# A fused RWKV5 and feed-forward kernel: packing the first chunks' k, staging w2 apart, and a new order

## The chip, the cores and the metric

The kernel runs on one core of one Trainium2 chip. A core has five engines with queues of their own: TensorE (matmul and transposes), VectorE, ScalarE, GpSimd, and SyncE, which mostly issues transfers; ScalarE issues transfers too. Each engine takes its instructions in the order of the program and waits on semaphores where another engine or a transfer has to come first. The metric is the time of the whole kernel on the device in microseconds, as the median of several runs; a profiled execution stands beside it.

## The reference

A linear attention with a decaying state (4 batches, 8 heads, 768 tokens, head size 48), then a layer norm and a feed-forward block with a residual over the 8 x 48 = 384 channels:

```python
for t in range(S):
    cur = einsum('bhd,bhe->bhde', u * k_t, v_t)
    y[:, :, t] = einsum('bhd,bhde->bhe', r_t, state + cur)
    state = w * state + einsum('bhd,bhe->bhde', k_t, v_t)
x = y as (B, S, 384)
xn = (x - mean(x)) / sqrt(var(x) + 1e-6) * g_ln
out = x + relu(xn @ w_ch1) @ w_ch2        # 384 -> 1536 -> 384
```

All inputs and the output are float32.

## The kernel before

The 768 tokens of each batch are cut into 6 chunks of 128, so there are 24 chunks. Inside a chunk the recurrence is done as attention: r is scaled by powers of w that grow with the token's place and k by powers that shrink, a matrix of products of r and k is masked to the lower triangle, and the state is carried from chunk to chunk. Each step of a chunk is a short function. For chunk i:

- LK, LV load k and v with a token to a partition (pieces of 192 bytes, one for each head and token); RA and RB load the two halves of r "packed", four tokens to a partition (pieces of 768 bytes), for chunks 0 to 17; LR loads r like k after that.
- SK and SR scale k and r into the bf16 tile `sc`, with the factors Fk and Fr (Fn for the later r). CV makes v bf16 (`vv`).
- TR transposes both on TensorE (four transposes for r, four for k), TCr and TCk copy the results from PSUM to `trs`; the copy of the packed r puts the tokens back in order. From chunk 14 on transfers transpose k (TKD), from 18 on both (TKR).
- Q multiplies the two turned tiles; AT makes the products of r and k for the eight heads, AM (or AMa and AMb, its halves) masks them on VectorE into `A`.
- S makes, on TensorE, the part with u and the state's new terms from `sc` and `vv`; CC copies the former, ZU and ZD form the decayed state Z. VB multiplies v by CC's result (`Vb`).
- Y puts together the output from Z and A; X adds Vb and sums over the channels; SQ and RS make the norm's factor; XN makes the normalised bf16 row.
- LT and XT turn it on TensorE for chunks 0 to 5; LT2 and LTD turn it by transfer later.

The feed-forward part works on groups of one or two chunks: UP is one PSUM bank's share of the first product (12 matmuls of 128 columns or 6 of 256), RL its ReLU into `hT` (on ScalarE or VectorE), DN a third of the second product (4 matmuls), OT the residual, STO the store. The last chunk's second product goes in two halves (DA, DB, OA, OB, SA, SB).

The weights arrive as float32. LW1 loads a third of w_ch1 into `w1_f`, SW scales it by the norm's g to bf16. LW2 loads a third of w_ch2 into the same memory, through w2_f, so it waits until SW has read it; CW makes it bf16. DU is a dummy matmul of 512 columns on TensorE, which keeps it busy while it has nothing else to do.

In the setup LC loads w, u and g_ln as rows, LN takes the logarithm, CT and CP turn the rows into columns, WBR and WBK spread the logarithms over the partitions by matmul, PW makes the exponents, and FK, FN and FR make the factors by exponentials on ScalarE, FR in four instructions.

The order is written out by hand as a long string, PLAN: each word names a step, its chunk (or part), and its engine (v VectorE, s ScalarE, g GpSimd, - the step's own; for transfers s is ScalarE's queue and - SyncE's). The steps are issued in that order, so every engine's queue has the order of its own words in the string. A tile with several buffers is a ring: chunk i takes buffer i modulo the number in SLOTS.

```python
for step in PLAN.split():
    name, i, e = step.split(",")
    steps[name](int(i), e)
```

Transfers signal their landing on eight semaphores in turn, so an issuing engine, before it issues, waits until the transfer that had the same semaphore before has landed.

Of the kernel before, what the change touches and what calls it, by code (L numbers as in the profile page):

```python
# [18 lines left out]
PLAN = """
MW,0,v LC,0,s TL,0,s MM,0,g DU,4,- LK,1,- LK,0,- MI,0,g DU,4,- DU,4,- RA,1,s DU,4,- LC,1,- LK,2,- RB,1,- LV,0,- LN,0,s  # L20
RB,0,s WBR,0,- DU,4,- BD,0,g LV,3,- DU,4,- PW,0,v MP,0,v FR,3,s FR,1,s WBK,0,- RA,0,s DU,4,- FR,2,s FR,0,s RA,2,s LV,1,-
LK,3,- DU,4,- DU,4,- LC,2,s DU,4,- SR,1,g DU,4,- DU,4,- FK,0,s SK,0,v FN,0,s SR,0,v RB,2,s LV,2,- SK,1,v LW1,1,s CT,0,-
TR,0,- LW1,0,- RA,3,s SK,2,v DU,4,- DU,4,- TCr,0,s LW1,2,- DU,4,- CP,0,v DU,4,- TCk,0,v UW,0,g CV,0,g TR,1,- Q,0,v SR,2,g
TCk,1,s DU,4,- S,0,- DU,4,- CC,0,s WL,0,s UGC,0,s RA,4,- DU,4,- SK,3,g CV,3,g TCr,1,s DU,4,- DU,4,- VB,0,g AT,0,- DU,4,-
SW,5,s TR,2,- CV,1,s Q,1,g ZU,0,v AMb,0,v AMa,0,v LK,4,- RB,5,- Y,0,- TCr,2,s RB,3,s X,0,v SW,4,s XN,0,s SW,3,v TCk,2,v
DU,4,- AT,1,- S,1,- DU,4,- CC,1,v DU,4,- VB,1,g AMa,1,v DU,4,- ZU,1,v RB,4,- DU,4,- LW2,1,- DU,4,- DU,4,- SW,2,s CV,2,s
SQ,0,s DU,4,- AMb,1,v LT,0,- SW,1,v Q,2,v DU,4,- AT,2,- Y,1,- SW,0,s SR,3,v XT,0,v DU,4,- LW2,0,s S,2,- TR,3,- UP,0,-
AMb,2,v DU,4,- SW,7,g SW,6,g CC,2,v TCr,3,s SW,8,s TCk,3,s DU,4,- AMa,2,v ZU,2,v RA,5,- DU,4,- DU,4,- RL,0,v X,1,v XN,1,s
UP,2,- LW2,2,- VB,2,g LK,5,- UP,1,- Q,3,g RL,2,v LV,4,- RB,6,- RA,6,- LT,1,- Y,2,- CW,1,s RL,1,s XT,1,v AT,3,- X,2,v
UP,17,- UP,16,- S,3,- AM,3,v XN,2,g CW,0,g RS,0,g RL,17,s LT,2,- Y,3,- RL,16,v CC,3,v XT,2,s UP,18,- SQ,1,s VB,3,v UP,32,-  # L30
RL,18,s X,3,v DN,0,- RL,32,s XN,3,v ZU,3,v SR,4,v UP,33,- CW,2,s CW,3,v LT,3,- UP,34,- RL,33,s XT,3,s SR,5,v DN,1,- SK,4,v
CW,5,s RL,34,s TR,4,- LK,6,- CW,4,v UP,48,- TCk,4,v SQ,2,s RB,8,s DN,2,- SK,5,g RS,1,g TCr,4,v UP,49,- OT,0,v RB,7,- Q,4,v
RA,7,s TR,5,- AT,4,- CV,4,v LV,5,- LK,7,- RA,8,- LV,6,- AM,4,v DN,4,- TCk,5,s S,4,- TCr,5,s RL,48,s SR,6,g DN,5,- RA,10,s
SQ,3,s Q,5,v Y,4,- CC,4,v SK,6,v DN,6,- ZU,4,v VB,4,g TR,6,- OT,1,v LK,8,- LV,7,- AT,5,- UP,50,- RS,3,g RL,49,s TCk,6,s
TCr,6,s X,4,v DN,8,- XN,4,g AM,5,v SR,7,g S,5,- LT,4,- DN,9,- XT,4,s RB,9,s CV,6,s RS,2,g LK,9,- RA,9,- AT,6,- SK,7,v
SQ,4,s UP,65,- DN,10,- RL,50,s Q,6,v CC,5,v CV,5,g SR,8,g RB,10,- LK,10,- S,6,- TR,7,- Y,5,- AM,6,v OT,2,v RL,65,s CC,6,v
VB,5,v UP,64,- RA,11,s TCr,7,s VB,6,g X,5,v DN,12,- STO,0,s CV,7,s TCk,7,v Y,6,- XN,5,g SQ,5,s ZU,6,v DN,13,- Q,7,v RL,64,s
LT,5,- RA,12,- SK,8,v RS,5,g AT,7,- S,7,- XT,5,v DN,14,- UP,66,- ZU,7,v SR,9,g X,6,v UP,81,- TR,8,- RL,66,s ZD,7,g AM,7,v
# [121 lines left out]

# [558 lines left out]
```

## Time and profile before

| | us |
|---|---|
| median of 3 runs | 155.74 |
| lowest, highest | 155.28, 156.29 |
| the profiled execution | 156.69 |
| its span, from first to last instruction | 154.9 |

The profile's times count from the start of the span, in us unless marked ns; the names of engines in it are PE for TensorE (PEld its weight loads), DVE for VectorE, ACT for ScalarE, POOL for GpSimd and SP for SyncE; SPq and ACTq are transfers issued by these. A row of the timeline has start, length, engine, line, operation, tiles with shapes and the number of instructions merged; square brackets say how long the engine had been idle before and what ended that. Rows can overlap by some tens of nanoseconds, because an instruction begins before the last has quite ended. A row of the groups has the busy time, the mean in ns, and after the second bar the idle time before these instructions with what ended it.

The whole span by engine: TensorE is busy 94% of it, VectorE 74%, GpSimd 58%, ScalarE 52%; transfers move 27.74 MB at 179 GB/s on average.

### The profile page before, as it was taken

The numbers are of one execution on the slowest core, as the hardware profiler recorded it, in microseconds if no ns is written. First come the engines' busy times: TensorE is split into PE (matmuls) and PEld (weight loads), VectorE is DVE, ScalarE is ACT, GpSimd is POOL, SyncE is SP. The second block draws the span as 40 slices with busy tenths as digits, with TensorE's granted clock in tenths as the row PEclk, the third lists the DMA queues.
The fourth block names the chain that finished last, engine by engine and source line by source line (L and its number), as shares of the span: only waits on it lengthen the run. The fifth ranks groups of instructions, "written<-read, shape, count | busy, mean of one in ns | idle before, by whom it ended". The sixth has DMA issues, their size and how long they took to land.

```text
span 154.9 us, 4408 instructions
## 1 busy us (share of the span) xinstructions
PE 145.7 (94%) x1744; PEld 110.4 (71%) x1744; DVE 115.4 (74%) x235; ACT 81.0 (52%) x183; POOL 89.3 (58%) x131
## 2 busy tenths in 40 slices
PE   4969899999999999999999999999999999799992
PEld 1326457897778877878887778688777878578881
DVE  0252499799899998997778989995984788496411
ACT  4321794686668387564996047862516631036130
POOL 5314763665288998796299596599634269403100
PEclk9999999999999999999999999999999999999999
DMA  4999989969989317969999969899998876521122
GB/s 92 231 242 305 368 223 295 276 147 223 189 199 254 78 30 174 230 190 207 225 142 208 138 153 223 204 222 112 253 213 179 161 165 106 146 78 30 51 102 102
DMA packets 82401, 27.74 MB, mean 179 GB/s; under 512 B 73035, under 2 KB 80846, under 8 KB 82382
## 3 DMA queue, kind: packets, MB, share of 16 engines
q1 hardware_dynamic: 77788, 21.96, 68.1%
q10 hardware_dynamic: 4594, 5.51, 11.8%
q8 instruction: 13, 0.21, 0.5%
q14 instruction: 6, 0.05, 0.1%
HBM read 18.88 MB, written 4.72 MB: 152 GB/s over the span
## 4 chain that ended last, share of the span: by engine, by line
PE 54%; DMA 13%; issue 10%; DVE 8%; POOL 7%; SPq 2%; ACT 2%; ACTq 1%; POOLq 0%; DVEq 0%
PE o L615 19%; PE hp L587 16%; PE o L304 4%; DMA rf<-in_r_dram 4%; DMA out_dram<-ot 4%; DMA trs<-sc 3%; PE at L435 3%; POOL sc L211 3%; DMA xT<-xn 3%; PE tr L415 2%; PE tr L419 2%; DVE sc L211 2%; PE y L516 2%; POOL rs L547 1%; PE s L479 1%
## 5 line engine op out<-in xcount | busy, mean ns | idle before, releaser
L587 PE MATMUL hp<-xT,w_sb 128*128 128x128 bf16 (+1 forms) x612 | 57.3, 242 | 1.0 <-DMA xT<-xn 0.8
L615 PE MATMUL o<-w_sb,hT 128*128 128x384 bf16 x276 | 55.6, 326 | 0.6 <-DVE ot L671 0.3
L587 PEld LDWEIGHTS <-w_sb 128*128 128x128 bf16 x612 | 48.6, 114 | 6.2 <-DMA xT<-xn 1.5
L603 ACT ACTIVATE hT<-hp 128x512 bf16<-128x512 f32 x55 | 32.4, 596 | 39.4 <-PE hp L587 36.9
L615 PEld LDWEIGHTS <-hT 128*128 128x128 bf16 x276 | 23.9, 97 | 11.1 <-issue 0.9
L445 DVE TENSOR_TENSOR A<-at,mask 128x1024 bf16<-128x1024 f32 (+1 forms) x27 | 29.5, 1097 | 1.6 <-PE at L435 1.3
L671 DVE SCALAR_TENSOR_TENSOR ot<-o,rs,x 128x384 f32<-128x384 f32 x23 | 14.1, 614 | 10.4 <-PE o L615 8.2
L498 POOL TENSOR_TENSOR Vb<-vf,cc 128x384 f32<-128x384 f32 x15 | 13.4, 891 | 13.4 <-DVE cc L208 10.3
L206 ACT COPY trs<-tr 128x512 bf16<-128x512 bf16 x22 | 12.4, 586 | 13.1 <-PE tr L419 13.1
L211 POOL TENSOR_TENSOR sc<-kf,Fk 128x384 bf16<-128x384 f32 x12 | 12.8, 1073 | 6.4 <-issue 2.9
L530 ACT ACTIVATE sqj<-x,sm 128x384 bf16<-128x384 f32 x24 | 14.8, 617 | 2.0 <-DVE x L523 1.6
L523 DVE SCALAR_TENSOR_TENSOR x<-y,Vb 128x384 f32<-128x384 f32 x24 | 13.2, 550 | 2.8 <-PE y L516 1.4
L211 POOL TENSOR_TENSOR sc<-rf,Fr 128x384 bf16<-128x384 f32 x13 | 13.7, 1057 | 2.3 <-DMA rf<-in_r_dram 2.3
L304 PE MATMUL o<-warm 128*128 128x512 bf16 x36 | 13.8, 508 | 1.1 <-DVE warm L259 1.1
L605 DVE TENSOR_SCALAR hT<-hp 128x512 bf16<-128x512 f32 x17 | 11.5, 686 | 2.4 <-PE hp L587 2.2
L547 POOL TENSOR_TENSOR rs<-rs,expo 128x1 f32<-128x1 f32 (+1 forms) x17 | 11.2, 662 | 1.4
L211 DVE TENSOR_TENSOR sc<-kf,Fk 128x384 bf16<-128x384 f32 x12 | 8.3, 701 | 3.1 <-ACT Fk L319 3.1
L211 POOL TENSOR_TENSOR Z<-ZS,WLZ 128x384 bf16<-128x384 f32 x8 | 8.3, 1043 | 3.6 <-DVE ZS L492 3.6
L211 POOL TENSOR_TENSOR q<-trs 128x512 bf16<-128x512 bf16 x7 | 8.4, 1200 | 3.3 <-DMA trs<-sc 2.4
L435 PE MATMUL at<-trs 48*128 48x128 bf16 x192 | 9.5, 219 | 0.3 <-DVE A L445 0.2
L435 PEld LDWEIGHTS <-trs 48*128 48x128 bf16 x192 | 5.4, 94 | 5.7 <-issue 3.8
L516 PE MATMUL y<-vv,A 128*128 128x48 bf16 x192 | 8.7, 183 | 0.5 <-DVE A L445 0.5
(90 smaller groups left out, 190.3 us busy)
## 6 DMA issues: line engine op xcount, KB each, us to landing
kf<-in_k_dram SPq DMA_DIRECT2D x24, 192.0 KB, 3.9
vf<-in_v_dram SPq DMA_DIRECT2D x24, 192.0 KB, 4.2
w_f<-in_moe_w_ch_dram SPq DMA_DIRECT2D x4, 768.0 KB, 6.3
out_dram<-ot ACTq DMA_DIRECT2D x12, 192.0 KB, 3.2
out_dram<-ot SPq DMA_DIRECT2D x11, 192.0 KB, 2.2
rf<-in_r_dram SPq DMA_DIRECT2D x21, 96.0 KB, 3.4
w_f<-in_moe_w_ch_dram ACTq DMA_DIRECT2D x2, 768.0 KB, 7.7
rf<-in_r_dram ACTq DMA_DIRECT2D x15, 96.0 KB, 3.5
```

The source lines that it names most:

```text
L211: engines[e].tensor_tensor(out=out, in0=in0, in1=in1, op=ALU.mult)
L304: nc.tensor.matmul(out=warm_ps[0][:], lhsT=warm[:], rhs=warm[:].unsqueeze(1).to_broadcast([P, 4, P]), start=True, stop=True)
L435: nc.tensor.matmul(out=t[:, par, q, :], lhsT=trs(i)[p0 : p0 + D, 1, q, :], rhs=trs(i)[p0 : p0 + D, 0, q, :], start=True, stop=True,)
L445: nc.vector.tensor_tensor(out=AA(i)[:, a:b].rearrange("p e q t -> p (e q) t"), in0=psum["at", i][:, a:b].rearrange("p e q t -> p (e q) t") ...
L498: engines[e].tensor_tensor(out=Vb(i)[:].rearrange("p (h d) -> p h d", h=H), in0=vf(i)[:], in1=cc(i)[:].unsqueeze(2).to_broadcast([P, H, D] ...
L523: nc.vector.scalar_tensor_tensor(out=xx(i)[:], in0=psum["y", i][:, :C], scalar=1.0, in1=Vb(i)[:], op0=ALU.mult, op1=ALU.add, accum_out=sm[ ...
L530: nc.scalar.activation(out=sqj[:], in_=xx(i)[:], func=ACT.Square, bias=sm[i][:], scale=-float(C), accum_out=sq[g][:, j : j + 1])
L547: nc.gpsimd.tensor_tensor(out=rs[g][:], in0=rs[g][:], in1=expo[:, :n], op=ALU.pow)
L587: nc.tensor.matmul(out=t[:, a * gw : (a + 1) * gw].rearrange("p (j t) -> p j t", j=size), lhsT=w1_sb[n][kc][:, fb::FB], rhs=xT(g)[:, :size ...
L603: nc.scalar.activation(out=o, in_=s, func=ACT.Relu)
L615: nc.tensor.matmul(out=psum["o", i][:, :C], lhsT=hT(g)[:, fk, j * P : (j + 1) * P], rhs=w2_sb[d][:, a, :], start=(fk == 0), stop=(fk == FK ...
L671: nc.vector.scalar_tensor_tensor(out=ot(i), in0=psum["o", i][:, :C], scalar=rs[g][:, j : j + 1], in1=xx(i)[:], op0=ALU.mult, op1=ALU.add,)
```

## The change

Four things are changed at once.

1. k of chunks 0 to 3 is loaded like r, packed, in two halves KA and KB. Its scaling uses a factor of its own, Fkp. After TR and TCk, k is there turned with its tokens in order, but `sc` holds it packed, and S needs it with a token to a partition; so TB turns it back on TensorE (four transposes) and KC copies it from PSUM over `sc` on VectorE.
2. The factors for packed tiles are made by a product on VectorE (ER for r, EK for k) and one exponential each on ScalarE (FR, FKP).
3. w2 has float32 tiles of its own, so its loads don't wait for w1's scaling. For that memory the rings of k, r and v have 10 buffers instead of 11.
4. PLAN is written anew. The weights' loads all go through SyncE's queue, the first after the loads of r, k and v for the first chunks, between those of the chunks 1 to 3. 31 dummies remain of 36. Work is spread differently: 17 SK on GpSimd instead of 12, 20 XN on ScalarE instead of 11 (none on GpSimd), and smaller moves. Chunk 8 is turned before chunk 7. In the last part chunk 23 overtakes chunk 22.

```diff
+K_PACKED = [0, 1, 2, 3]
-SLOTS = {'kf': 11, 'rf': 11, 'vf': 11, 'sc': 3, 'vv': 4, 'trs': 3, 'q': 2, 'A': 2, 'cc': 4, 'Z': 6, 'ZS': 2, 'Vb': 3, 'x': 13, 'xn': 4, 'xT': 4, 'hT': 4, 'ot': 4}
+SLOTS = {'kf': 10, 'rf': 10, 'vf': 10, 'sc': 3, 'vv': 4, 'trs': 3, 'q': 2, 'A': 2, 'cc': 4, 'Z': 6, 'ZS': 2, 'Vb': 3, 'x': 13, 'xn': 4, 'xT': 4, 'hT': 4, 'ot': 4}
 PLAN = """
...
+MW,0,v LC,0,s TL,0,s LV,1,- RB,0,- LV,0,- DU,4,- KA,1,- LC,2,s DU,4,- DU,4,- DU,4,- LC,1,s DU,4,- LV,2,- RA,0,- LK,4,-
+RB,2,s DU,4,- MI,0,g LN,0,s KB,0,s KA,0,- KB,1,- DU,4,- CT,0,- WBR,0,- BD,0,v MP,0,v PW,0,v ER,0,v CP,0,s RB,1,s LW1,0,-
+RA,1,s CV,1,g DU,4,- CV,0,g EK,0,v DU,4,- WBK,0,- DU,4,- MM,0,g CV,2,g UGC,0,s FR,0,s FKP,0,s KB,2,s FN,0,s KA,2,- SR,0,v
+LW1,2,- SK,0,v FK,0,s WL,0,s SK,1,v DU,4,- KB,3,- RA,2,- DU,4,- DU,4,- DU,4,- TR,0,- DU,4,- DU,4,- DU,4,- DU,4,- TCk,0,v
+TCr,0,v DU,4,- SW,1,s RB,4,s Q,0,v DU,4,- TB,0,- AT,0,- SR,1,g UW,0,g KC,0,v S,0,- CC,0,s TR,1,- DU,4,- AMb,0,v AMa,0,v
...
+    w2_fl = [const.tile([P, FK // NW, C], FP32, name=f"w2_f{n}") for n in range(NW)]
...
+        nc.vector.tensor_scalar(out=pow_k4[:], in0=pow_r[:], scalar1=-1.0, scalar2=-1.0, op0=ALU.mult, op1=ALU.add)
+    def spread(out, powers):
+        nc.vector.tensor_tensor(
+            out=out[:], in0=psum["lnr"][:, :P].rearrange("p (e x) -> p e x", e=2)[:, :, :D].unsqueeze(1).to_broadcast([P, TP, 2, D]),
+            in1=powers[:].unsqueeze(2).unsqueeze(3).to_broadcast([P, TP, 2, D]), op=ALU.mult,
+        )
+    def ER(i, e):
+        spread(Fr, pow_r)
+    def EK(i, e):
+        spread(Fkp, pow_k4)
     def FR_(i, e):
-        nc.scalar.activation(
-            out=Fr[:, i], in_=psum["lnr"][:, :P].rearrange("p (e x) -> p e x", e=2)[:, :, :D], func=ACT.Exp,
-            scale=pow_r[:, i : i + 1],
-        )
+        nc.scalar.activation(out=Fr[:], in_=Fr[:], func=ACT.Exp)
+    def FKP(i, e):
+        nc.scalar.activation(out=Fkp[:], in_=Fkp[:], func=ACT.Exp)
     def w2_f(n):
-        return w1_f[n][:].rearrange("p k f -> p (k f)").rearrange("p (a c) -> p a c", c=C)
+        return w2_fl[n][:]
...
+    def packed(tile_, src, i, e, par):
+        b, c = divmod(i, NCH)
+        issuer(e).dma_start(
+            out=tile_[:, par].rearrange("p t d -> p (t d)"),
+            in_=src[b, :, c * L : (c + 1) * L, :].rearrange("(q e) (k t) d -> e k q (t d)", e=2, t=TP)[par],
+        )
+    def KA(i, e):
+        packed(kfp(i), k, i, e, 0)
+    def KB(i, e):
+        packed(kfp(i), k, i, e, 1)
     def SK(i, e):
+        if i in K_PACKED:
+            times(e, sckp(i)[:, :, :, :D], kfp(i).rearrange("p e t d -> p t e d"), Fkp[:])
+        else:
             times(e, sck(i)[:, :, :D], kf(i)[:], Fk[:])
...
     def TCk(i, e):
+        if i in K_PACKED:
+            copy(e, trs(i)[:, 1].rearrange("p q (k t) -> p q k t", t=TP), psum["tr", i][:, HP:].rearrange("p t (k q) -> p q k t", q=HP))
+        else:
             copy(e, trs(i)[:, 1], psum["tr", i][:, HP:])
+    def TB(i, e):
+        t = psum["tb", i] = ps.tile([P, 2 * HP, P], BF16, name="tr")
+        for q in range(HP):
+            nc.tensor.transpose(out=t[:, q, :], in_=trs(i)[:, 1, q, :], identity=ident[:])
+    def KC(i, e):
+        copy(e, sck(i).rearrange("p h d -> p (h d)"), psum["tb", i][:, :HP].rearrange("p q t -> p (q t)"))
```

More of the change, by code (lines that the diff above doesn't have):

```diff
@@ L21 @@
[L21 to L30, printed above, removed]
@@ L73 @@
+OB,23,v STO,21,- SB,23,- DA,0,- STO,20,s DA,1,- DA,2,- OA,23,v SA,23,s STO,22,-
 """
```

109 lines of the change are left out of this document (59 added, 50 removed).

## The prediction, made before the run

> **What bounds the kernel now.** I read the page's shares first, then the table of stretches, then the timeline of TensorE and VectorE, then VectorE's groups between 33 and 80 us.
>
> ```profile
> PE 145.7 (94%) x1744; PEld 110.4 (71%) x1744; DVE 115.4 (74%) x235; ACT 81.0 (52%) x183; POOL 89.3 (58%) x131
> 0.00:10.00 10.00, 7.83 (x16) 2.28 (x16) 2.41 (x13) 3.79 (x8) 4.10 (x18) 1.00 0.84 182
> 10.00:20.00 10.00, 8.28 (x71) 5.08 (x71) 4.14 (x9) 4.35 (x11) 5.21 (x8) 1.00 1.01 315
> 20.00:30.00 10.00, 9.28 (x135) 6.89 (x134) 9.53 (x24) 7.08 (x15) 5.15 (x6) 1.00 0.85 264
> 30.00:40.00 10.00, 9.73 (x150) 8.37 (x150) 9.22 (x19) 6.86 (x16) 5.35 (x8) 1.00 0.91 202
> ```
>
> The columns of the last four lines are TensorE, its weight loads, VectorE, ScalarE, GpSimd (busy us), then granted clock, DMA share and GB/s. The 74% of VectorE is an average that misleads. Until 20 us the transfers are at 84 to 101% and every engine has holes; from 20 to 40 us VectorE is busy 9.2 to 9.5 us of ten while TensorE is filled, at first partly with dummies. So the front (to 20 us) can be shortened by transfers or by order; the next stretch only by giving VectorE less or earlier work; and after that TensorE's own work decides.
>
> ```profile
> 11.26 0.57 PE L252 MATMUL s<-idr,rows 11*128 11x11 f32 x2 [1.23 <-issue]
> 11.76 0.61 PE L415 MATMUL tr<-ident,sc 128*128 128x128 bf16 x4
> 12.58 1.91 PE L304 MATMUL o<-warm 128*128 128x512 bf16 x4
> 17.30 0.40 PE L435 MATMUL at<-trs 48*128 48x128 bf16 x8
> 20.41 1.67 PE L304 MATMUL o<-warm 128*128 128x512 bf16 x7
> 25.00 0.83 PE L587 MATMUL hp<-xT,w_sb 128*128 128x128 bf16 x12
> 32.87 0.08 DVE L523 DVE_READ_ACCUMULATOR x<-y,Vb 128x1 f32 x1
> 37.44 0.81 PE L615 MATMUL o<-w_sb,hT 128*128 128x384 bf16 x4 [0.21 <-DVE w_sb L208]
> 78.69 1.23 DVE L445 TENSOR_TENSOR A<-at,mask 128x1024 bf16<-128x1024 f32 x1 [0.57 <-PE at L435]
> 82.53 0.36 PE L516 MATMUL y<-vv,A 128*128 128x48 bf16 x8
> 151.33 0.49 PE L630 MATMUL o<-w_sb,hT 128*128 128x192 bf16 x4
> ```
>
> These are my marks: the first transposes (step TR of chunk 0) at 11.76, its AT at 17.30, the first UP at 25.00, X of chunk 3 finished at 32.95, the mask of chunk 13 (the tenth since) from 78.69 to 79.92, Y of chunk 13 at 82.53, and TensorE's last matmul ending at 151.82. What follows it, 3.1 us to the end of the span, is the last half tile and its store, in both plans.
>
> **The change, part by part.** *Loads.* The k of chunks 0 to 3 comes in two halves, in pieces four tokens long instead of one.
>
> ```profile
> kf<-in_k_dram SPq DMA_DIRECT2D x4, 192.0 KB, 3.5
> rf<-in_r_dram ACTq DMA_DIRECT2D x6, 96.0 KB, 3.5
> w_f<-in_moe_w_ch_dram SPq DMA_DIRECT2D x2, 768.0 KB, 7.6
> ```
>
> (Transfers issued before 12 us, median us to landing.) A whole k takes 3.5 us to land and half an r takes 3.5 as well, so latency, not size, dominates and two halves are no slower than one k. From both sides: the packed k of a chunk saves at most the difference between 182 GB/s (the stretch to 10 us) and 315 (the next), 196.6 KB times that, 0.46 us, and costs at most one more issue. SyncE issues in order, and each load waits until an earlier one has landed: KA of chunk 0 stands there behind three v, both halves of chunk 0's r, half a k and chunk 4's k; KB goes through ScalarE's queue behind the small constants. I let both be issued by 6 us and land by 9.5; up to 10 us this costs nothing, as the next paragraph but one shows. The w1 loads, which stood behind all first loads, now stand between them: the first after KB of chunk 1, at about 7.5, so landed by about 15 with its 7.6 us. The third waits on SyncE for that landing, and behind it queue the last halves of chunk 3's k and r, its v, and w2. At 15 to 18, landed by 22, they are in time for SK of chunk 3, which GpSimd reaches after chunk 2's Vb, SR and three more products of about 1 us, at about 22; the first UP needs w1 scaled after 20. I count 0, and 1 us if these loads come late (in the range). *w2 staged apart.* The only wait for w2 in the front is the 0.21 us at 37.44: the new tiles are worth at most that, and I take 0. They cost no engine time.
>
> *Factors.* ER and EK on VectorE (two products of 128x384) and two exponentials on ScalarE replace four small ones; they run between 6 and 9.5 us, while VectorE is three quarters idle (2.41 of the first 10 us) and the r and k are still on their way: 0.
>
> *TensorE's order.* Before TR of chunk 0 now stand seven dummies, CT, WBR, two dummies, WBK and five dummies; behind it six more dummies, then TB, AT.
>
> ```profile
> 1.10 1.89 PE L304 MATMUL o<-warm 128*128 128x512 bf16 x4 [1.10 <-DVE warm L259]
> 4.05 0.76 PE L231 MATMUL y<-ln_rows,sel 4*128 4x129 f32 x2 [1.07 <-ACT ln_rows L221]
> 5.71 1.64 PE L237 MATMUL s<-ln_bd,ones 4*128 4x384 f32 x2
> ```
>
> A dummy takes 0.43 us there (four in 1.91, of which the last 0.2 is its draining). Seven from 1.10 end at 4.2. CT waits for three small loads, which now all go through ScalarE's queue; WBR, which waited for the first of them alone, ran at 4.05, and two more issues of about half a microsecond make it 5.1. Then 0.57 + 0.76 + 2 x 0.43 + 1.57 + 5 x 0.43 = 5.9 gives TR at 11.0, against 11.76; this is why r and k may land until 10. TR takes 0.9 (the row at 11.76 and as much again for k), six dummies 2.6, TB as four transposes 0.4: AT at 14.9. Before, the first mask began 0.48 after AT's 17.30, at 17.78; so now at 15.4. The start of VectorE's chain is 2.4 us earlier.
>
> *VectorE to X of chunk 3.* From that mask on its queue holds 6 half masks, 1 whole one, 4 X, 3 KC, 4 ZU, 3 XT, 3 hT evictions, 2 Q, 2 turned copies, and one each of XN, SR and Vb with two cc. By the means of the rows below (a half mask as half of a whole one, KC as a turned copy, a cc at 0.16) that is 3.7 + 1.2 + 2.2 + 1.5 + 2.2 + 1.1 + 2.0 + 1.0 + 1.0 + 2.1 = 18.0 us, and 16.0 after taking off 0.06 for each of the 33, since one starts before the last has ended (below, the quoted groups fill 43.3 us and those left out some 5, in 47.0 us that hold 3.7 us of waits: 5 us of overlap over some 83 instructions). KC is a new wait in this queue: it stands for TB's four transposes, and the masks and X of the same chunk queue behind it, with ScalarE's XN and TensorE's LT after X; S waits for KC in turn. I add 0.4 for each of the four round trips (the waits of a kind in the rows below sum to 0.3 to 0.8): 15.4 + 16.0 + 1.6 = 33.0 for X of chunk 3, against 32.95. The 2.4 us are gone: KC costs 1.5 with its waits 3, and before VectorE did part of the same work in holes.
>
> *VectorE from there to the mask of chunk 13.*
>
> ```profile
> L445 DVE TENSOR_TENSOR A<-at,mask 128x1024 bf16<-128x1024 f32 x10 | 12.2, 1219 | 0.9 <-PE at L435 0.7
> L671 DVE SCALAR_TENSOR_TENSOR ot<-o,rs,x 128x384 f32<-128x384 f32 x8 | 4.9, 613 | 0.6 <-PE o L615 0.5
> L211 DVE TENSOR_TENSOR q<-trs 128x512 bf16<-128x512 bf16 x10 | 4.8, 479 | 0.4 <-ACT trs L206 0.4
> L523 DVE SCALAR_TENSOR_TENSOR x<-y,Vb 128x384 f32<-128x384 f32 x8 | 4.4, 552 | 0.9 <-PE y L516 0.8
> L211 DVE TENSOR_TENSOR sc<-kf,Fk 128x384 bf16<-128x384 f32 x5 | 3.2, 649 | 0.0
> L208 DVE COPY trs<-tr 128x512 bf16<-128x512 bf16 x6 | 3.0, 504 | 0.6 <-PE tr L419 0.6
> L211 DVE TENSOR_TENSOR sc<-rf,Fr 128x384 bf16<-128x384 f32 x3 | 2.5, 831 | 0.0
> L492 DVE TENSOR_TENSOR ZS<-s,Z 128x384 f32<-128x384 f32 x4 | 2.2, 548 | 0.3 <-PE s L479 0.3
> L208 DVE CAST w_sb<-w_f 128x768 bf16<-128x768 f32 x2 | 1.9, 954 | 0.0
> L498 DVE TENSOR_TENSOR Vb<-vf,cc 128x384 f32<-128x384 f32 x3 | 1.6, 548 | 0.0
> L605 DVE TENSOR_SCALAR hT<-hp 128x512 bf16<-128x512 f32 x2 | 1.4, 683 | 0.0
> L538 DVE TENSOR_SCALAR xn<-x,sm 128x384 bf16<-128x384 f32 x2 | 0.8, 418 | 0.0
> L208 DVE COPY xT<-tr 128x384 bf16<-128x384 bf16 x1 | 0.4, 358 | 0.0
> ```
>
> (Busy us, mean ns, idle before.) Both plans do ten masks and eight X in this stretch. The new one has 2 Q, 2 SK, 3 turned copies, 2 XN, 1 ot, 1 w2 cast, 1 ZU and 1 ZD fewer, and 3 Vb, 2 XT, 1 SR and 1 cc more: by these means -0.96 -1.30 -1.51 -0.84 -0.61 -0.95 -1.10 +1.65 +0.72 +0.83 +0.2 = -3.9, and -3.5 with 0.06 of overlap for each of the six. Of the waits in these rows, those for TensorE sum to 0.7 + 0.5 + 0.8 + 0.6 + 0.3 = 2.9 us. TensorE has, from its first DN at about 31.5 to Y of chunk 13, 21 UP, 21 DN and ten chunks' attention, some 40 us by the rows that follow, so it could be at that Y at 71.5, ahead of VectorE; then part of the 2.9 falls away. They can go entirely or not at all, and I take 1.7. Before, the stretch took 79.92 - 32.95 = 47.0. Now 33.0 + 47.0 - 3.5 - 1.7 = 74.8, and Y of chunk 13 at 75.2.
>
> *TensorE from Y of chunk 13.* Before, 82.53 to 151.82 is 69.3 us with 2.6 us of slack ahead of it (79.92 to 82.53), so the new order has used up that slack by pulling attention ahead of the feed-forward part, and owes the rest later: 3 UP, 5 DN, 1 Y and 1 TR more.
>
> ```profile
> 109.44 0.82 PE L587 MATMUL hp<-xT,w_sb 128*128 128x256 bf16 x6
> 110.09 0.81 PE L615 MATMUL o<-w_sb,hT 128*128 128x384 bf16 x4
> 110.74 0.33 PE L508 MATMUL y<-Z,trs 128*128 128x96 bf16 x4
> 111.12 0.81 PE L615 MATMUL o<-w_sb,hT 128*128 128x384 bf16 x4
> ```
>
> From start to start an UP and a DN take 0.65 each and a Y 0.38; a TR is about 0.2. That is 5.8, so 75.1 us. TensorE ends at 75.2 + 75.1 = 150.3, 1.5 us sooner. All TB and the last dummies lie ahead of the mark at Y, in TensorE's slack. The rings of ten instead of eleven inputs, SK moved to GpSimd (12 to 17 there, 58% busy) and XN to ScalarE (11 to 20, 52% busy) have room and I count 0.
>
> The profiled execution took 156.69 us for a span of 154.9, and the median shown is 155.74. 155.2 of 156.69, times 155.74, is 154.3, with 153.0 to 155.6 for this case (1.3 for how much of the 2.9 goes).
>
> **The clock.** The row at 12.58 has a dummy at 0.43 us, the row at 20.41 at 0.24, while the granted clock stands at 1.00 in all stretches: TensorE reaches its full rate only at about 16 us. My sum has it so again, at the slow rate until AT of chunk 0, and gives 154.3. The Trainium skill ("TensorE: Matmul & The Clock Gate", Part 1) says that the array runs at half rate until it has been busy for about 3.4 us, and falls back after an idle window of that length. The two rates agree with these rows, though the granted clock doesn't show them; by that rule, 31 dummies for 36 could leave the array slow for longer, and the sum would be that of the third rival below.
>
> **The rivals.** *More is won.* VectorE needs no wait in either stretch: X of chunk 3 at 31.4 and 2.9 taken off instead of 1.7. TensorE ends at 31.4 + 47.0 - 3.5 - 2.9 + 0.4 + 75.1 = 147.5, 4.3 us sooner: 151.4. For it: TensorE's slack of 3 us against VectorE in the new plan. Against it: even in the busiest ten microseconds above VectorE was idle for 0.47.
>
> *Slower: VectorE waits more between 33 and 75 us.* This stretch is now in series with TensorE's remainder, because the slack of 2.6 us is gone: each microsecond that VectorE waits there is one at the end.
>
> ```profile
> L211 POOL TENSOR_TENSOR sc<-kf,Fk 128x384 bf16<-128x384 f32 x12 | 12.8, 1073 | 6.4 <-issue 2.9
> ```
>
> The place is X, which needs Vb, which stands in GpSimd's queue with the SK: five more of them are there in the new plan, 5 x 1.07 = 5.4 us, and behind X on VectorE wait the hT evictions and the next mask. If the 2.9 us of waits stay, the end is 0.2 late; from 1.4 us more it is over 1% slower. If half of the 5.4 shows at X, 2.7 more, it is 2.9 late, 158.6. For it: chunk 8 is turned before chunk 7, so two chunks' SK, SR and Vb meet in that queue. Against it: GpSimd is free for 4.65 to 4.85 us of each ten from 20 to 40 us.
>
> *The clock stays low.* If TensorE runs at half rate until the first UP, which I expect at about 22 us, the eleven groups from S of chunk 0 to Y of chunk 1 take 0.2 to 0.4 us more each, some 3 us; VectorE's queue hides about half, the 1.5 us won are lost, and the time is 155.7, no change. The longest hole I expect ahead of it is 0.9 us (4.2 to 5.1), shorter than those in the rows above.
>
> **How the numbers follow.** About 1% is what a measurement of this kernel can tell from no change, 154.2 to 157.3. The forecast has 0.50, of which 0.27 lies below 154.2 and 0.23 above; more is won 0.13; slower 0.25; the clock 0.12, of which 0.02 is below. That is 0.42 faster, 0.33 the same, 0.25 slower. The range reaches from the gain in full (151.4) to the slower case at 158.4, and leaves out about a tenth above and half of that below.
>
> **What would show it.** In the new profile: AT of chunk 0 near 15 us; X of chunk 3 done between 32 and 34; VectorE's stretch from there to the mask of chunk 13 about 42 us with under 3 us of waits; Y of chunk 13 right behind that mask and at about 75; TensorE without holes from there. I am wrong if X of chunk 3 is done before 31 (the front gives more than I think), if Y of chunk 13 has slack ahead of it (then VectorE doesn't pace), or if holes before xT appear after 110 us, where the last three groups' UP follow closely on their transposes.

## The result, and the profile after

| | before | after |
|---|---|---|
| median of 20 executions each, us | 156.14 | 154.96 |
| lowest to highest, us | 155.28 to 157.24 | 153.23 to 156.61 |
| ratio after to before, 95% interval | | 0.9888, 0.9862 to 0.9915 |
| the profiled execution, its span, us | 156.69, 154.9 | 156.04, 153.6 |

The change makes the kernel 1.1% faster. 154.3 was predicted. Ratios leave out executions that are over 1.5% above the fastest of the same kernel, of which the changed kernel has more than the one before (its profiled execution is one of them), so marks inside the profiles are compared below and not their totals.

From the page of the kernel after, the shares by engine; from its table of stretches, the first 40 us (TensorE, weight loads, VectorE, ScalarE, GpSimd, granted clock, DMA share, GB/s):

```profile
PE 144.1 (94%) x1755; PEld 110.6 (72%) x1755; DVE 113.4 (74%) x238; ACT 84.3 (55%) x183; POOL 90.1 (59%) x133
0.00:10.00 10.00, 7.80 (x18) 2.86 (x19) 3.99 (x16) 3.35 (x8) 3.78 (x19) 1.00 0.78 168
10.00:20.00 10.00, 7.96 (x83) 4.76 (x81) 6.42 (x15) 5.09 (x12) 5.77 (x8) 1.00 1.00 337
20.00:30.00 10.00, 9.87 (x165) 8.14 (x163) 9.09 (x22) 7.72 (x17) 8.85 (x12) 1.00 0.96 308
30.00:40.00 10.00, 9.33 (x151) 7.60 (x149) 9.32 (x19) 7.50 (x15) 5.54 (x10) 1.00 0.79 180
```

The shares look as before. What moved is GpSimd from 20 to 30 us, 5.15 to 8.85 of ten, and TensorE there, 9.28 to 9.87 with fewer dummies. The marks that the prediction used, from the timeline of the kernel after (start, length, engine, line, operation):

```profile
11.14 0.63 PE L450 MATMUL tr<-ident,sc 128*128 128x128 bf16 x4
13.98 0.40 PE L481 MATMUL at<-trs 48*128 48x128 bf16 x8
21.95 0.83 PE L633 MATMUL hp<-xT,w_sb 128*128 128x128 bf16 x12
31.33 0.81 PE L661 MATMUL o<-w_sb,hT 128*128 128x384 bf16 x4
34.13 0.07 DVE L569 DVE_READ_ACCUMULATOR x<-y,Vb 128x1 f32 x1
73.81 1.22 DVE L491 TENSOR_TENSOR A<-at,mask 128x1024 bf16<-128x1024 f32 x1
75.47 0.36 PE L562 MATMUL y<-vv,A 128*128 128x48 bf16 x8
149.32 1.15 PE L676 MATMUL o<-w_sb,hT 128*128 128x192 bf16 x12
```

| | before | predicted | after |
|---|---|---|---|
| TR of chunk 0 | 11.76 | 11.0 | 11.14 |
| AT of chunk 0 | 17.30 | 14.9 | 13.98 |
| first UP | 25.00 | about 22 | 21.95 |
| first DN | 33.05 | about 31.5 | 31.33 |
| X of chunk 3 done | 32.95 | 33.0 | 34.20 |
| mask of chunk 13 done | 79.92 | 74.8 | 75.03 |
| Y of chunk 13 | 82.53 | 75.2 | 75.47 |
| from there to TensorE's end | 69.3 | 75.1 | 75.0 |
| TensorE's end | 151.82 | 150.3 | 150.47 |

All but one of these came out within a microsecond; X of chunk 3, at 34.20, came 1.2 us late. That does not show that the reasons were right. The two tables of stretches below, before first and then after, are cut at X of chunk 3, at Y of chunk 13 and at TensorE's end:

```profile
32.95:82.53 49.58, 49.37 (x678) 39.79 (x676) 44.37 (x88) 35.20 (x80) 36.88 (x47) 1.00 0.82 180
82.53:151.82 69.29, 68.06 (x798) 53.51 (x795) 52.07 (x98) 28.68 (x67) 36.37 (x50) 1.00 0.78 152
```

```profile
34.20:75.47 41.27, 40.60 (x581) 33.09 (x579) 37.70 (x80) 29.45 (x64) 25.82 (x33) 1.00 0.77 170
75.47:150.47 75.00, 73.70 (x848) 58.19 (x845) 51.82 (x102) 35.17 (x80) 42.31 (x57) 1.00 0.74 152
```

In the stretch that I gave to VectorE, TensorE is busy for 49.37 of 49.58 us before and for 40.60 of 41.27 after. VectorE has 5.2 us of holes before and 3.6 after. So either engine could be the one that paces, and TensorE has the better claim. In the prediction it was the other way round. The experiments begin there.

### The profile page after: what moved, and what is told of

It reads as the page before. It is cut to its first block, busy times and chain, and to the rows that moved or that the text cites. A ratio compares the mean times of both kernels' runs of the same rounds, so it can differ in the third digit from the quotient of the medians.

```text
span 153.6 us, 4451 instructions
## 1 busy us (share of the span) xinstructions
PE 144.1 (94%) x1755; PEld 110.6 (72%) x1755; DVE 113.4 (74%) x238; ACT 84.3 (55%) x183; POOL 90.1 (59%) x133
## 4 chain that ended last, share of the span: by engine, by line
PE 69%; DMA 15%; DVE 6%; POOL 5%; issue 2%; ACT 1%; ACTq 1%; DVEq 0%; POOLq 0%
PE hp L633 26%; PE o L661 25%; DMA kf<-in_k_dram 4%; DMA vf<-in_v_dram 4%; DMA trs<-sc 4%; PE at L481 4%; PE y L562 2%; DMA xT<-xn 2%; PE y L554 2%; PE tr L450 2%; POOL sc L218 2%; PE s L525 2%; PE tr L454 2%; DVE A L491 1%; POOL q L218 1%
## 5 line engine op out<-in xcount | busy, mean ns | idle before, releaser
L649 ACT ACTIVATE hT<-hp 128x512 bf16<-128x512 f32 x54 | 31.5, 596 | 27.9 <-PE hp L633 27.4
L544 POOL TENSOR_TENSOR Vb<-vf,cc 128x384 f32<-128x384 f32 x14 | 11.8, 846 | 16.1 <-DVE cc L215 9.4
L213 ACT COPY trs<-tr 128x512 bf16<-128x512 bf16 x24 | 13.7, 584 | 10.3 <-PE tr L454 6.8
L218 POOL TENSOR_TENSOR sc<-kf,Fk 128x384 bf16<-128x384 f32 x15 | 15.4, 1028 | 3.3 <-PE s L525 3.0
L582 ACT ACTIVATE xn<-x,sm 128x384 bf16<-128x384 f32 x20 | 12.2, 615 | 8.5 <-DVE x L569 6.0
L218 POOL TENSOR_TENSOR sc<-rf,Fr 128x384 bf16<-128x384 f32 x12 | 12.7, 1066 | 5.6 <-DMA rf<-in_r_dram 5.6
L311 PE MATMUL o<-warm 128*128 128x512 bf16 x31 | 11.9, 505 | 1.1 <-DVE warm L266 1.1
L218 DVE TENSOR_TENSOR q<-trs 128x512 bf16<-128x512 bf16 x19 | 9.3, 489 | 2.3 <-DMA trs<-sc 2.0
L590 POOL TENSOR_SCALAR rs<-sq 128x1 f32<-128x1 f32 (+1 forms) x17 | 4.8, 282 | 10.3 <-ACT sqj L576 9.2
L215 POOL CAST vv<-vf 128x384 bf16<-128x384 f32 x14 | 7.4, 526 | 5.8 <-DMA vf<-in_v_dram 5.8
L218 POOL TENSOR_TENSOR q<-trs 128x512 bf16<-128x512 bf16 x5 | 6.2, 1239 | 6.3 <-ACT trs L213 3.4
```

Of the source, the lines that this page charges most:

```text
L213: nc.scalar.copy(out=out, in_=in_)
L218: engines[e].tensor_tensor(out=out, in0=in0, in1=in1, op=ALU.mult)
L582: nc.scalar.activation(out=xn(i), in_=xx(i)[:], func=ACT.Identity, bias=sm[i][:], scale=-float(C))
L649: nc.scalar.activation(out=o, in_=s, func=ACT.Relu)
```

## The experiments

Twelve kernels ran, four at a time on one chip, with the kernel before beside them. Ratios are to that. Each has one profile, and the profiles of one program differ: the changed kernel's two have X of chunk 3 to Y of chunk 13 in 41.27 and 41.17 us, but the stretch behind it in 75.00 and 73.41.

**More work for VectorE, in both kernels.** A step JV, six times, behind the masks of chunks 4, 5, 6, 9, 10 and 12:

```diff
+    junk = const.tile([P, C], FP32, name="junk")
+    def JV(i, e):
+        nc.vector.tensor_tensor(
+            out=junk[:], in0=Fk[:].rearrange("p h d -> p (h d)"), in1=Fn[:].rearrange("p h d -> p (h d)"), op=ALU.mult
+        )
-... AM,4,v ...
+... AM,4,v JV,4,v ...
```

> The kernel before with six more VectorE products of 128x384 f32 (about 0.55 us each by the ZS rows, 3.3 us in all), whose results nobody reads, one behind each of the masks of chunks 4, 5, 6, 9, 10 and 12, all in the stretch in which VectorE is busiest. Theory (VectorE paces that stretch, but the plan of before leaves 2.6 us of slack ahead of Y of chunk 13, and TensorE's remainder sets the end): the mask of chunk 13 ends about 3 us later, at 83, Y of chunk 13 starts at 83.2 instead of 82.5, and the time rises by 0.2 to 0.9 us (ratio to the kernel before 1.001 to 1.006). Rival A (VectorE's chain sets the end in this kernel too): +2.5 to +3.3 us, ratio 1.016 to 1.021. Rival B (the products fill VectorE's waits): the mask stays within 1 us and the time within 0.3 us.

> The changed kernel with the same six products behind the same six masks. Theory (the new order has used up the slack, so VectorE's stretch from X of chunk 3 to the mask of chunk 13 is in series with TensorE's remainder): mask and Y of chunk 13 come 2.3 to 3.3 us later, at about 78, and the time rises by as much, from 154.9 to 157.2 to 158.2; ratio to the kernel before 1.007 to 1.013. Rival A (VectorE does not pace; the 3.5 us of its waits in that stretch swallow the work): Y of chunk 13 stays within 0.7 us of 75.5 and the time within 0.5 us of the changed kernel, ratio 0.986 to 0.992. Rival B (TensorE's remainder takes up part of it, because masks later than chunk 13's were early): Y later by 3, the end by 1 to 2.

| | ratio | 95% interval |
|---|---|---|
| before, with six JV | 1.0124 | 1.0077 to 1.017 |
| after, with six JV | 0.998 | 0.993 to 1.003 |

Against 1 and 0.9888 the work costs 1.2% and 0.9%, 1.9 and 1.4 us. The theory wanted nearly nothing in the first kernel and the whole in the second. Both kernels pay a part, and about the same part; by the medians of all executions it is 1.4% in each. The kernel before with JV, from X of chunk 3 to Y of chunk 13:

```profile
32.08:83.71 51.63, 49.94 (x677) 39.70 (x675) 48.64 (x94) 34.98 (x80) 36.27 (x47) 1.00 0.76 172
```

This stretch grew by 2.05 us, from 49.58, and TensorE's idle time in it from 0.21 to 1.69. So the 2.6 us that the theory took for slack did not take the work up. The changed kernel with JV, cut as above, and its group of JV on VectorE between the same marks:

```profile
32.81:75.24 42.43, 41.35 (x581) 32.96 (x578) 41.71 (x85) 29.22 (x63) 27.56 (x33) 1.00 0.75 167
75.24:149.22 73.98, 73.48 (x848) 58.14 (x845) 51.90 (x102) 35.44 (x80) 41.55 (x56) 1.00 0.73 154
```

```profile
L733 DVE TENSOR_TENSOR junk<-Fk,Fn 128x384 f32<-128x384 f32 x6 | 4.8, 808 | 0.0
```

The six products take 4.8 us (I had written 3.3), and VectorE is now busy for 41.71 of 42.43 us. The stretch grew by 1.16 us, from 41.27; most of the rest went into VectorE's holes, which fell from 3.57 to 0.72 (its other work took 0.8 us less). So VectorE is close behind TensorE in this stretch, but work on it is not in series: it costs about a quarter of its length inside the stretch. This profile doesn't show where the 1.4 us of the ratio come from, since behind Y of chunk 13 it is 1.02 us shorter than the first profile of the changed kernel.

**More work for TensorE, in the same stretch.** Four UP are done twice:

```diff
-        for a in range(nf):
+        for a in list(range(nf)) * (2 if i in (48, 64, 65, 81) else 1):
```

> The changed kernel with four of its UP steps (48, 64, 65 and 81, all between Y of chunk 4 and Y of chunk 13) done twice, the second time over the same psum: 4 x 0.65 = 2.6 us of TensorE work that changes nothing else. Theory, new after the first runs (TensorE is full from about 31 us on, and the end is the sum of its work): Y of chunk 13 and the end 2.3 to 2.7 us later, the time at 157.3 to 157.7; ratio to the kernel before 1.003 to 1.009. Rival, the step of the prediction (VectorE's stretch sets Y of chunk 13, TensorE waits there for its mask): TensorE has its waits to spend, the time rises by under 1 us; ratio 0.986 to 0.994.

The table of stretches of this kernel:

```profile
34.53:78.47 43.94, 43.27 (x628) 35.76 (x626) 38.12 (x80) 29.34 (x64) 26.00 (x33) 1.00 0.74 164
78.47:152.08 73.61, 73.36 (x848) 58.20 (x845) 52.04 (x102) 35.38 (x80) 41.62 (x56) 1.00 0.78 154
```

The stretch went from 41.27 to 43.94 us: 2.67 for 2.6 us of TensorE work, all of it. For VectorE's 4.8 it was 1.16. TensorE paces up to Y of chunk 13, and the step of the prediction falls. Behind Y the stretch is 1.4 us shorter than 75.00, but not shorter than the 73.41 of the changed kernel's second profile, so it can't be put down to the added work. The ratio, 0.9977 (0.9929 to 1.0026), is 0.9% above 0.9888, 1.4 us, about half of what the theory wanted; by the medians of all executions it is 1.2%, 1.8 us. How much of the 2.67 reaches the end is not settled closer than that.

**Without packing; with chunk 1's r early.** The changed kernel waits on GpSimd. GpSimd's timeline there, and X of chunk 0 on VectorE:

```profile
13.58 1.27 POOL L218 TENSOR_TENSOR sc<-rf,Fr 128x384 bf16<-128x384 f32 x1 [5.58 <-DMA rf<-in_r_dram]
14.81 0.47 POOL L218 TENSOR_TENSOR uwI<-cols 48x4 bf16<-48x4 f32 x2
15.76 0.99 POOL L218 TENSOR_TENSOR sc<-kf,Fkp 128x384 bf16<-128x384 f32 x1 [0.48 <-DMA kf<-in_k_dram]
16.72 0.83 POOL L544 TENSOR_TENSOR Vb<-vf,cc 128x384 f32<-128x384 f32 x1
17.58 0.56 DVE L569 SCALAR_TENSOR_TENSOR x<-y,Vb 128x384 f32<-128x384 f32 x1 [1.80 <-POOL Vb L544]
```

SR of chunk 1 waits 5.58 us for half of that chunk's r. Behind it in GpSimd's queue stand UW (a small step that makes S's factor with u), SK of chunk 2, which waits another 0.48 us for a packed half of that chunk's k, and only then Vb of chunk 0, for which VectorE waits 1.80 us. The wait that ends last is the one for k. In the second profile of the same kernel SR comes 0.48 us earlier and Vb 0.63 later:

```profile
13.10 0.99 POOL L218 TENSOR_TENSOR sc<-rf,Fr 128x384 bf16<-128x384 f32 x1 [4.82 <-DMA rf<-in_r_dram]
16.39 1.00 POOL L218 TENSOR_TENSOR sc<-kf,Fkp 128x384 bf16<-128x384 f32 x1 [1.87 <-DMA kf<-in_k_dram]
17.35 0.83 POOL L544 TENSOR_TENSOR Vb<-vf,cc 128x384 f32<-128x384 f32 x1
```

The last half of chunk 2's k goes through ScalarE's queue, behind chunk 1's r; in the first profile it is issued at 8.79 and lands after 6.8 us. Two kernels take a part of this away; the first leaves out TB, KC, EK and FKP and loads k as the kernel before does:

```diff
-K_PACKED = [0, 1, 2, 3]
+K_PACKED = []
-KA,1,- ... KB,0,s KA,0,- KB,1,- ... TB,0,- AT,0,- ... KC,0,v S,0,-
+LK,1,- ... LK,0,- ... AT,0,- ... S,0,-
```

```diff
-LV,2,- RA,0,- LK,4,- ... KA,0,- KB,1,- ... RB,1,s LW1,0,- RA,1,s ... LW1,2,- ... SR,1,g UW,0,g
+RB,1,- LV,2,- RA,0,- ... KA,0,- KB,1,- RA,1,- ... LW1,0,- ... LW1,2,- LK,4,- ... UW,0,g SR,1,g
```

> The changed kernel without the packing of k: chunks 0 to 3 load k as before, in one transfer each at the place of the first half; the turning back (TB on TensorE, KC on VectorE) and the repeated factors (EK and its two exponentials) are left out; the order is otherwise the new one. Theory (packing only adds VectorE work in the front: four KC with their waits, 1.5 to 3 us by the prediction, and brings transfers nothing that is needed): X of chunk 3 ends 1 to 3 us sooner, at 31 to 33, Y of chunk 13 at 73 to 74.5, and the time falls by 0.8 to 2.5 us to 152.4 to 154.1; ratio to the kernel before 0.976 to 0.987. Rival A (the packing pays by its transfers: whole k in small pieces land later, the first transposes come over 1 us later): X of chunk 3 later, time up by 0.5 to 2 us. Rival B (another wait sets X of chunk 3, chunk 1's half r on GpSimd or Vb): no change within 0.5 us, ratio 0.986 to 0.992.

> The changed kernel with chunk 1's two half r loaded earlier, both through SyncE's queue ahead of the first w1 third, with chunk 4's k moved behind the last w1 third, and with GpSimd's small factor step UW ahead of SR of chunk 1 instead of behind it. Theory (in the profile of the changed kernel GpSimd waited 5.58 us for that r, S of chunk 0 0.96 us for UW and X of chunk 0 1.80 us for Vb; they are why X of chunk 3 came 1.2 us later than predicted, and VectorE is in series from there): X of chunk 3 ends 0.8 to 2 us sooner, Y of chunk 13 by as much, time 153.0 to 154.2, ratio to the kernel before 0.979 to 0.987. Rival A (what VectorE does not wait for there it waits for behind it, TR of chunk 2 and the shared transfers): X of chunk 3 within 0.4 us of 34.2, time within 0.5 us of the changed kernel. Rival B (SyncE's loads of w1 and k come later for it): TR of chunk 0 or the first UP over 0.5 us later, time up.

| | ratio | 95% interval | X of chunk 3 done | first DN |
|---|---|---|---|---|
| k not packed | 0.9784 | 0.9731 to 0.9838 | 32.36 | 29.98 |
| r of chunk 1 early | 0.9791 | 0.9731 to 0.9852 | 32.77 | 29.91 |

Both are about 1% faster than the changed kernel, and in both Vb of chunk 0 comes earlier. The second moves more than r: with r gone from ScalarE's queue, chunk 2's k is issued 0.77 us earlier, and its SK starts at 14.04 instead of 15.76, so this run doesn't tell the one load from the other. GpSimd in the kernel with r early:

```profile
9.78 0.99 POOL L222 TENSOR_TENSOR sc<-rf,Fr 128x384 bf16<-128x384 f32 x1 [0.27 <-DMA rf<-in_r_dram]
14.04 1.00 POOL L222 TENSOR_TENSOR sc<-kf,Fkp 128x384 bf16<-128x384 f32 x1 [3.27 <-DMA kf<-in_k_dram]
15.20 0.83 POOL L548 TENSOR_TENSOR Vb<-vf,cc 128x384 f32<-128x384 f32 x1 [0.16 <-ACT cc L217]
```

**Both at once, with and without late dummies; UW alone.** The edits are those above; the third kernel also drops the six DU behind TR of chunk 2, and the fourth has no packing and only `UW,0,g` moved ahead of `SR,1,g`.

> The changed kernel with both mendings of the first runs at once: k of chunks 0 to 3 not packed (no TB, KC, EK), and chunk 1's r early through SyncE's queue with UW ahead of SR of chunk 1 and chunk 4's k behind the last w1 third. Alone they gave 0.978 and 0.979 of the kernel before. Theory (the two take away different things: TensorE's four TB and VectorE's four KC, 1.5 us of TensorE each chunk's work summed; and the wait for UW and Vb in chunks 0 and 1): they add for the most part, ratio 0.966 to 0.974, time near 151. Rival (both only bring the first chunks forward, and transfers then set the pace): no better than the better of the two, ratio 0.976 to 0.981.

> The changed kernel without packing, with chunk 1's r early and UW ahead, and without the six dummies behind TR of chunk 2. The same with these dummies had 0.980. Theory (TensorE's sum sets the end, dummies behind 20 us are paid): 6 x 0.22 = 1.3 us less TensorE time, of which half or more shows; ratio 0.972 to 0.977. Rival (as in the kernel before without its late dummies: holes take their place): 0.978 to 0.983 and as much idle time more on TensorE between 20 and 31 us as dummies less.

> The changed kernel without the packing of k, and with GpSimd's small UW ahead of SR of chunk 1; the loads of r stay where the change put them. Without packing alone the ratio was 0.978. Theory (S of chunk 0 waits for UW behind SR, which waits for chunk 1's r; UW ahead of it takes 0.5 to 1 us off chunk 0's way, but chunk 1's r still comes at 13.4): first X earlier by 0.5 us or more, X of chunk 3 by 0 to 0.5, ratio 0.974 to 0.979. Rival (the wait moves to Vb, which stands behind SR of chunk 1 on GpSimd all the same): no difference to the unpacked kernel, 0.977 to 0.981.

| | ratio | 95% interval | first DN |
|---|---|---|---|
| both | 0.9804 | 0.9755 to 0.9854 | 29.81 |
| both, no late dummies | 0.9775 | 0.9712 to 0.9838 | 29.86 |
| not packed, UW ahead | 0.9754 | 0.9692 to 0.9816 | 30.82 |

They don't add. The rival held: either mending brings Vb of chunk 0 to about 15 us, and the first DN to about 29.9, and the second finds nothing left. What the six dummies cost lies inside the intervals, and the first DN did not move. The kernel with UW ahead has the lowest ratio, but no earlier first DN than its neighbours, so its profile doesn't show UW to be the cause. In this profile and in that of the kernel that only leaves the packing out, TensorE's granted clock is at 0.50 from about 18 to 21 us; what that costs them no run shows.

**Dummies alone, in both kernels.** Without the six (after) or the thirteen (before) late DU:

> The changed kernel without the six dummies that stand behind TR of chunk 2 (from 21 us on; 25 of 31 stay). Theory (TensorE is full from there on, so what it does for nothing there is paid at the end): first UP, first DN and the end earlier by the dummies' time, 6 x 0.22 = 1.3 us; time 153.5 to 154.0, ratio to the kernel before 0.980 to 0.984. Rival A (VectorE's chain sets the front and the stretch to 75 us, TensorE waits instead of working for nothing): holes of about the same sum on TensorE between 21 and 31 us, time within 0.4 us of the changed kernel. Rival B (without them TensorE falls back to the slow rate of the first stretch): matmuls of 0.4 us and more behind the gap, time up by 1 us or more.

> The kernel before without the thirteen dummies that stand behind AT of chunk 1 (from 20 us on; 23 of 36 stay), and with nothing of the change. Theory (TensorE's sum sets the end here too): up to 13 x 0.22 = 2.9 us can be had, less what TensorE then waits for; with half of them covering waits, 1 to 2 us, ratio 0.987 to 0.994, about the gain of the whole change. Rival A (the waits that the dummies cover are all real): holes in their place, ratio 0.997 to 1.003. Rival B (slow rate): ratio over 1.005.

Before: 1.0013 (0.998 to 1.0045), first DN at 33.62 instead of 33.05. The thirteen dummies covered waits, and holes took their place: TensorE's idle time up to the first DN went from 4.67 to 7.96 us. Without them the granted clock also fell, to 0.50 from about 21 to 27 us, where the kernel before has 1.00:

```profile
24.00:26.00 2.00, 2.00 (x27) 1.83 (x24) 2.00 (x6) 0.19 (x1) 0.62 (x1) 0.50 0.91 255
```

The mean granted clock is 0.976 to 0.989 in all twelve executions of this kernel, and below 0.99 in 3 of 29 of the kernel before. So nothing of the gain can be had there by leaving out dummies alone: they also kept TensorE's clock up. After: 0.9806 (0.976 to 0.9853), which looks like the theory's gain, but the first DN is at 31.66 and the idle time up to it 6.11 us, against 31.33 and 4.38 in the first profile of the changed kernel. The profile shows no place where such a gain would come from. By the medians of all executions, 155.85 and 157.15, the ratio is 0.992, which the changed kernel has by its medians too (154.96 and 156.14), so this gain is not shown.

**w2 in w1's memory again, and the changed kernel once more.**

```diff
-        return w2_fl[n][:]
+        return w1_f[n][:].rearrange("p k f -> p (k f)").rearrange("p (a c) -> p a c", c=C)
-LW2,0,- AMa,1,v ...
+AMa,1,v ... SW,2,s LW2,0,- ...
```

> The changed kernel once more, for a second trace of it on the chip of the other three: ratio to the kernel before 0.986 to 0.992, X of chunk 3 to Y of chunk 13 41.3 us within 0.5, from there to TensorE's end 74.0 to 75.0. Whatever differs from the first trace by more than this lies in the front, where the instant at which TensorE's matmuls become fast has differed between executions by several microseconds. If the ratio is outside 0.983 to 0.995, comparisons across calls cannot carry differences of half a per cent.

> The changed kernel with w2 back in w1's staging memory (each w2 third loads into the tile of its w1 third, its load issued behind the last scaling of that third), everything else as in the changed kernel. Theory (the prediction's: w2 apart is worth at most the 0.21 us that TensorE waited for w2 in the kernel before): landing of w2's first third later by up to 5 us, first DN within 0.3 us, time within 0.4 us of the changed kernel. Rival (the new order needs w2 earlier, casts of w2 and the input loads queued on SyncE behind the waiting w2 load come late): DN of chunk 0 or TR of chunk 4 wait, time up by 1 us or more, ratio 0.995 or higher.

The changed kernel again had 0.9884 (0.9838 to 0.993), so the ratio came out the same a second time. With w2 in w1's memory it is 0.9798 (0.9739 to 0.9856). The two intervals overlap a little. w2 apart brings nothing, as predicted; whether it costs something isn't settled, since in the two profiles first DN (31.97 and 31.96) and TensorE's end (149.42 and 149.16) are nearly the same.

**One table for all.** From each timeline: the start of Vb of chunk 0 on GpSimd, the first DN, TensorE's end; and TensorE's busy time between the last two.

| kernel | Vb of chunk 0 | first DN | difference | TensorE's end | busy between |
|---|---|---|---|---|---|
| before | 17.74 | 33.05 | 15.31 | 151.82 | 117.33 |
| before, JV | 16.30 | 32.18 | 15.88 | 151.92 | 117.69 |
| before, no late dummies | 16.21 | 33.62 | 17.41 | 151.79 | 116.91 |
| after | 16.72 | 31.33 | 14.61 | 150.47 | 117.17 |
| after, again | 17.35 | 31.97 | 14.62 | 149.42 | 116.72 |
| after, JV | 15.33 | 29.94 | 14.61 | 149.22 | 117.71 |
| after, UP twice | 17.01 | 31.66 | 14.65 | 152.08 | 119.50 |
| after, no late dummies | 17.03 | 31.66 | 14.63 | 150.02 | 117.06 |
| after, w2 shared | 17.35 | 31.96 | 14.61 | 149.16 | 116.79 |
| after, r early | 15.20 | 29.91 | 14.71 | 148.84 | 117.33 |
| not packed | 14.77 | 29.98 | 15.21 | 147.39 | 116.73 |
| not packed, UW | 15.73 | 30.82 | 15.09 | 149.58 | 116.87 |
| both | 15.41 | 29.81 | 14.40 | 149.10 | 116.93 |
| both, no late dummies | 15.32 | 29.86 | 14.54 | 148.73 | 117.20 |

In all six profiles with packing and with r where the change put it, the first DN follows Vb of chunk 0 by 14.61 to 14.65 us. Vb need not be the cause itself: Q of chunk 1, SR of chunk 2 and Vb of chunk 1 stand behind it in GpSimd's queue and move with it (SR of chunk 2 starts 2.7 us after it in each of the six). In three of the six (after, UP twice, w2 shared) the chain of work that ended last runs back from TR of chunk 2 through this queue to the half of chunk 2's k. In the plan of before there is no such link: with Vb about 1.5 us sooner its first DN came 0.87 sooner in one profile and 0.57 later in the other, where the granted clock fell. From the first DN on TensorE works for 117.2 us within 0.6 (the repeated UP add 2.3), in every plan, and what is left up to its end is idle time of 0.4 to 2.4 us. The time is the instant of the first DN, plus a constant, plus those few holes. The two JV kernels show how much of that is chance, as their fronts are those of before and after: the one has its first DN at 32.18 instead of 33.05; in the other chunk 1's r came at 11.3 instead of 13.6, SK of chunk 2 started at 14.38 instead of 15.76, and the first DN came at 29.94.

## Why the prediction was right, step by step

- *TR and AT of chunk 0.* Right within 0.2 us for TR. AT came 0.9 earlier than predicted: the six dummies ahead of it (2.6 us predicted) took 1.82, since TensorE became fast among them, at about 13 us. The clock rival wanted the opposite.
- *X of chunk 3, 33.0.* 34.20 measured. The loads were counted at 0 to 1 us, and on SK of chunk 3, which was not what waited. The price was paid in GpSimd's queue, by Vb of chunk 0 behind SR of chunk 1 and SK of chunk 2. That two halves are no slower than one k, 3.5 us, did not hold for the last half of chunk 2, which took 6.8. For the added waits of KC the prediction had named what is queued behind them. For loads that come later, which do the same to GpSimd, it had not.
- *Packing costs VectorE 1.5 to 3 us in the front.* With r early, the kernels with packing and without have their first DN at 29.91 and 29.81. By X of chunk 3, at 32.77 and 32.19, KC and TB cost 0.6 us, and 0.1 at the first DN. That the unpacked kernel is faster than the changed one fits SR of chunk 1 starting at 10.83 instead of 13.58, and SK of chunk 2 at 13.81 instead of 15.76; why that half r lands earlier without packing wasn't tried by itself.
- *VectorE from X of chunk 3 to the mask of chunk 13: 41.8.* 40.8 measured, by terms that were off. X of chunk 3 was 1.2 us late and this stretch 1.0 short, so that the mark behind it came out is partly luck. Some of VectorE's groups between these marks in the kernel after, to be read against those in the prediction:

```profile
L491 DVE TENSOR_TENSOR A<-at,mask 128x1024 bf16<-128x1024 f32 x10 | 12.1, 1215 | 0.1
L717 DVE SCALAR_TENSOR_TENSOR ot<-o,rs,x 128x384 f32<-128x384 f32 x7 | 4.3, 615 | 2.4 <-PE o L661 2.4
L218 DVE TENSOR_TENSOR q<-trs 128x512 bf16<-128x512 bf16 x8 | 3.4, 429 | 0.2 <-ACT trs L213 0.2
L218 DVE TENSOR_TENSOR sc<-rf,Fr 128x384 bf16<-128x384 f32 x4 | 2.2, 551 | 0.3 <-DMA rf<-in_r_dram 0.3
L215 DVE CAST w_sb<-w_f 128x768 bf16<-128x768 f32 x1 | 0.5, 543 | 0.0
```

  The counts are as predicted, but single instructions are shorter (Q 479 to 429 ns, SR 831 to 551, the cast of w2 954 to 543), which gave more than the 3.5 us counted. The waits, from which 1.7 us were to go, hardly went (VectorE is idle there for 3.6 us, 4.2 before): they moved from the mask and X to OT, which waits 2.4 us for TensorE's DN. That is the sign of the engine that paces: VectorE waits for TensorE.
- *The step that failed* is the sentence that TensorE has "some 40 us" from its first DN to Y of chunk 13 and "could be at that Y at 71.5, ahead of VectorE", and with it "this stretch is now in series with TensorE's remainder". It took the count of UP, DN and chunks and a round figure. TensorE's row between the two marks in the kernel after:

```profile
31.33:75.47 44.14, 43.47 (x631) 35.41 (x629) 40.56 (x86) 32.14 (x70) 28.19 (x37) 1.00 0.76 168
```

  43.47 us of work from 31.33 on lead to 74.8, and with 0.67 of idle time to 75.47, where VectorE's sum had led too. The plan is balanced there, so a sum over the wrong engine gave the right mark, which is luck. The "2.6 us of slack" of before was likewise other TensorE work that stood ahead of that Y.
- *TensorE's remainder, 75.1:* measured 75.0. The counting of UP, DN, Y and TR was right, and the end, 150.3 predicted and 150.47 measured, follows.
- *More is won* wanted X of chunk 3 at 31.4 and didn't happen. *VectorE waits more* had a mechanism on GpSimd's queue with Vb in it, which did occur, but in chunk 0 and not between 33 and 75 us, and at 1.2 us on X of chunk 3.

So the 1.35 us between the two profiles are the first DN, 1.72 sooner, less 0.37 behind it (118.77 to 119.14 us, through holes of 1.44 and 1.97). Packing is worth nothing by the runs, w2 apart nothing or less, and leaving out dummies alone, in the kernel before, nothing. What is left for the first DN is the new order with its loads, and the factors' products; these weren't tried in smaller parts, so which of them brings the 1.1% stays open.

A piece of the gain is lost outside the span. Where the changed kernel was measured a second time, the median span fell from 155.1 to 152.4 us, 2.7, and the median time from 156.92 to 155.56, 1.4. What lies around the span is 1.82 us in the median before and 2.41 after (1.80 without packing and with UW ahead). What it is no run shows.

## What to carry to other kernels

Before an engine is named as the one that paces a stretch, its busy time and that of the other full engine are to be read between the same two marks; a round figure for one of them can turn the answer, and a balanced plan hides the error. Two small experiments then tell: a few microseconds of useless work on each engine, and how far the next mark moves. When a plan moves loads, every instruction that waits for one must be looked up with what stands behind it in that engine's queue: here one product of chunk 0 stood behind loads of chunks 1 and 2, and sending chunk 1's r earlier, which let chunk 2's k come earlier too, gained about as much again as the whole change. A ratio is also to be read with how many executions it rests on.
